# Top-32 attention and a quick-GELU MLP on one core: the end rows of a batch move in the work list, and MLP units are queued differently

## The chip, the core and the metric

The kernel runs on one core of a Trainium2 chip. The time is the device time of one execution in microseconds (us); the figure compared is the median of several runs. Every time below comes from the kernel before the change: its three timed runs, and one profiled execution.

The engines are named as in the profile: PE multiplies matrices (PEld is its weight load), DVE and POOL work elementwise on vectors, ACT applies functions and copies, SP issues nearly all DMA transfers from one queue, in program order.

## What is computed

Attention over 8 batches, 8 heads, 576 rows and 64 columns, in which only the 32 largest scores of a row count; then an MLP from 512 to 2048 to 512 columns over all 4608 rows.

```python
scores = scale * np.matmul(q, k.transpose(0, 1, 3, 2))
kth = np.partition(scores, -32, axis=-1)[..., -32:-31]
scores = np.where(scores >= kth, scores, -1e9)
attn = softmax(scores)
x = np.matmul(attn, v)          # then (B,H,S,D) -> (B*S, H*D)
h = x @ w_in
g = h * (1.0 / (1.0 + np.exp(-1.702 * h)))
out = g @ w_out
```

## The kernel before

**Slots.** The attention is a list of 144 slots (line 293), 18 for each of the 8 batches. A slot is 128 query rows of two heads (a head pair `hp`, of four). 576 rows are four full tiles of 128 and an end of 64, so a batch has 16 full slots, (tile, head pair), and two end slots; an end slot holds the last 64 rows of two head pairs at once. Before, every batch has its first three tiles (12 slots), then its two end slots, then its last tile (4 slots).

A slot passes these steps: `scores` on PE (line 303); `copy_scores` on ACT (319); `pair_up` and `topk` on DVE, called by `find` (328, 336, 956), which is most of DVE's time; `bounds` on POOL (361); `mask` and `exps` on ACT (375, 381); `normalize` on POOL (406); `split` (442), which ACT starts and SP ends by writing `rows` to DRAM; `turn_by_dma` (450), an SP transfer that brings the rows back transposed as `pt`; `values_at` on PE (504); `x_of` on ACT (522), which writes a part of the MLP's input `xT`. `pt` has two buffers, the scores `sc` four.

**Blocks and units.** When the last head pair of a tile is through, a block of 128 MLP rows is ready (`finish_x`, 534). The ends of two batches make one block, ready in the odd batch. There are 36 blocks of four units. A unit passes `hidden` on PE (562, called H below), `tanh` on ACT (581), `gate` (593), `combine` (610) and `project` on PE (657, called P below). `combine` makes four sums, `s1` to `s4`; `project` multiplies 28 small products, of which the first four read only the gated values and the fifth reads `s2`. Each of these steps has a queue, and a call takes the oldest unit that waits there, or does nothing. While slots run, `gate` and `combine` are POOL's; after the last slot they are DVE's.

**The order by hand.** Nothing is scheduled for the program: each engine runs its instructions in the order in which the code emits them. From slot 13 on, one call of `two_slots(n)` (1018) emits two slots' worth of work; n is odd, and "pair n" below is that call. On PE a full pair is H, H, scores(n+2), P, P, the values of slots n-3 and n-2, scores(n+3). After the last pair, `last_units` (1091) emits H, tanh, gate, combine and P of what is left.

**Due times.** `later` (733) holds work for a slot: loads of q, k and v, and the preparation of the next batch's q and k. `begin(0)` and `begin(1)` emit what is due at slots n and n+1; `prepare_some` emits preparations. From batch 2 on a preparation, `prepare_by_dma` (259), is a copy on ACT, four SP transfers to DRAM and, at `turns` (1044), one SP transposing transfer into `qk_t` (277). Batch 1 is prepared on PE (`prepare_by_pe`, 285). `READY`, `FETCH` and `VALUES` (741 to 745) say by head pair how many slots from the start of a batch this is due. One `load_v` (208) is three SP transfers.

Of the kernel before, what the change touches and what calls it, by code (L numbers as in the profile page):

```python
# [30 lines left out]
def kernel(  # L31
# [32 lines left out]
    NP = H // 2  # L64
# [24 lines left out]
    STEADY = PAIRED + 2  # L89
# [23 lines left out]
    ps_t = pool("ps_t", 2, space=PSUM)  # L113
# [118 lines left out]
    def turn_qk_ends(b, hp, ends):  # L232
        nc.tensor.transpose(ends, loaded.pop((b, hp))[1][:, 0, :, :], ident[:])
# [16 lines left out]
    def new_pair(b, hp):  # L250
        both = qkt.tile([P, 2 * S + TAIL], F32, name="qk_t")
        qT[b, hp], kT[b, hp] = both[:, 0:S], both[:, S : 2 * S + TAIL]
        return both
# [5 lines left out]
    def prepare_by_dma(b, hp):  # L259

        t = loaded.pop((b, hp))[2]
        halves = prp.tile([P, 2 * NF + 1, 2, P], U16, name="halves", tag="pr")
        words = t[:].rearrange("p c j d -> p c (j d)").bitcast(U16)
        nc.scalar.copy(out=halves[:], in_=words.rearrange("p c (e h) -> p c h e", h=2))
        rows = apart_qk.tile([2 * (S + TAIL), 2, P], U16, name="qk_rows")
        main = rows[:].rearrange("(g r) h e -> g r h e", g=2)[:, 0:FULL, :, :]
        for g in range(2):
            nc.sync.dma_start(
                main[g].rearrange("(t p) h e -> p t (h e)", p=P),
                halves[:, g * NF : (g + 1) * NF, :, :].rearrange("p t h e -> p t (h e)"),  # L270
            )
        nc.sync.dma_start(rows[FULL : FULL + P, :, :], halves[:, 2 * NF, :, :])
        nc.sync.dma_start(rows[2 * S : 2 * S + TAIL, :, :], halves[TAIL:P, 2 * NF, :, :])

        def turn():
            both = new_pair(b, hp)
            nc.sync.dma_start_transpose(
                out=both[:].bitcast(U16), in_=rows[0 : 2 * S + TAIL, :, :].rearrange("c h e -> (c h) e")
            )

        turns.append(turn)

    turns = []

# [8 lines left out]
    slots = []  # L293
    for b in range(B):

        full = [(b, t, (hp, hp)) for t in range(NF) for hp in range(NP)]
        ends = [(b, NF, (hp, hp + 1)) for hp in range(0, NP, 2)]
        slots += full[: -NP] + ends + full[-NP:]
    N = len(slots)
    PER = N // B  # L300
    st = [{} for _ in slots]
# [67 lines left out]
    def exponentials(n, between=lambda: None):  # L369

        mask(n)
        between()
        exps(n)
# [188 lines left out]
    def hidden(into=None):  # L562
        if not ready:
            return
        x = ready[0]
        fs, x.left = x.left[:G], x.left[G:]
        ph = ps_t.tile([P, G * P], F32, name="ph", tag="tp")[:] if into else both_banks[:, 0, :]
        for i, f in enumerate(fs):
            for c in range(CC):
                nc.tensor.matmul(  # L570
                    ph[:, i * P : (i + 1) * P],
                    lhsT=win[:, c, f * P : (f + 1) * P],
                    rhs=xs[:, x.place, c, :],
                    start=(c == 0),
                    stop=(c == CC - 1),
                )
        to_gate.append((ph, fs, x))
        if not x.left:
            free.append(ready.pop(0).place)

    def tanh(aside):

        if to_gate:
            ph, fs, x = to_gate.pop(0)
            th = thp.tile([P, G * P], F32, name="th")
            nc.scalar.activation(th[:], ph, AF.Tanh, scale=0.851 / RAISE)
            if aside:
                h = thp.tile([P, G * P], F32, name="h", tag="th")
                nc.scalar.copy(out=h[:], in_=ph)
                ph = h[:]  # L590
            gated.append((th, ph, fs, x, aside))
# [18 lines left out]
    def combine():  # L610

        if not to_combine:
            return
        th, h, fs, x, aside = to_combine.pop(0)
        if x.whole:
            return to_project.append((th, None, fs, x))
        sums = h if aside else thp.tile([P, G * P], F32, name="sums", tag="th")[:]
        engine = nc.gpsimd if aside else nc.vector
        g = th[:].rearrange("p (h c i r) -> p h c i r", h=2, c=2, i=2)
        s = sums.rearrange("p (s c r) -> p s c r", s=4, c=2)  # L620
        a11, a12, a21, a22 = g[:, 0, :, 0, :], g[:, 1, :, 0, :], g[:, 0, :, 1, :], g[:, 1, :, 1, :]
        s1, s2, s3, s4 = [s[:, i, :, :] for i in range(4)]
        engine.tensor_tensor(out=s1, in0=a21, in1=a22, op=ALU.add)
        engine.tensor_tensor(out=s2, in0=s1, in1=a11, op=ALU.subtract)
        engine.tensor_tensor(out=s4, in0=a12, in1=s2, op=ALU.subtract)
        engine.tensor_tensor(out=s3, in0=a11, in1=a21, op=ALU.subtract)
        to_project.append((th, (a11, a12, a22, s1, s2, s3, s4), fs, x))
# [25 lines left out]
    def sum_weights(count):  # L653
        for _ in range(min(count, len(summing))):
            summing.pop(0)()
# [66 lines left out]
    def merge_all(engine=nc.gpsimd):  # L722
        while merging:
            merging.pop(0)(engine)
# [10 lines left out]
    def at(n, fn, *args):  # L735
        later.setdefault(n, []).append((fn, args))
# [1 line left out]

    READY = (-13, -9, -5, -1)
    READY_1 = (-5, -5, -3, -1)
    FETCH = (-17, -13, -9, -5)
    FETCH_1 = (-11, -6, -4, -3)
    VALUES = (0, 1, 2, 3)
    by_slot = dict(enumerate([2, 2, 3, 3, 3, 3, 3, 3, 3, 3, 3, 1]))
    for n in by_slot:
        first = sum(map(len, list(by_slot.values())[:n]))
# [10 lines left out]
    for b in range(1, B):  # L759
        for hp in range(NP):  # L760
            if b > 1:
                for i, name in enumerate("qk"):
                    at(b * PER + FETCH[hp] + i, load, name, b, hp)
                at(b * PER + READY[hp], prepare_by_dma, b, hp)
            else:
                at(b * PER + FETCH_1[hp], load_both, b, hp)
                at(b * PER + READY_1[hp], prepare_by_pe, b, hp)
            at(b * PER + VALUES[hp], load_v, b, hp)
    unfinished = []
    early = []  # L770
    finished = []
# [4 lines left out]
    def may_project(waiting):  # L776

        return len(to_project) > waiting and len(finished) >= NG * CC + to_project[0][2][-1] + 1
# [188 lines left out]
    def project_one():  # L967
        if may_project(0):
            project(True)
# [48 lines left out]
    def two_slots(n):  # L1018

        begin, prepare_some = dues(n)  # L1020
        aside = n < N
        filling = n < STEADY + 8
        if live(n - 1):
            exponentials(n - 1)
        if n == STEADY or n > STEADY + 4:
            prepare_some()
        hidden(ps_t)
        hidden(ps_t)
        tanh(aside)
        if live(n + 2):  # L1030
            scores(n + 2)
        project_one()
        merge_all()
        combine()
        project_one()
        find(n, 8)
        if live(n - 1):
            normalize(n - 1)
            split(n - 1)
        gate()  # L1040
        begin(0)
        if live(n - 1):
            turn_by_dma(n - 1)
        while turns:
            turns.pop(0)()
        if live(n + 2):
            copy_scores(n + 2)
        if live(n):
            bounds(n)
            mask(n)  # L1050
        combine()
        sum_weights(4)
        if live(n):
            exps(n)
        tanh(aside)
        prepare_some()
        held = [m for m in (n - 3, n - 2) if live(m)]
        o = ps_t.tile([P, 4, P], F32, name="o", tag="tp") if held else None
        ends = [(b, hp, o[:, 2 + i, :]) for i, (b, hp) in enumerate(second_part)]
        second_part.clear()  # L1060
        for what in ends:
            turn_qk_ends(*what)
        for i, m in enumerate(held):
            values_at(m, o[:, i, :])
        if filling and held:
            x_of(held, o)
        for what in ends:
            copy_qk_ends(*what)
        if filling:
            begin(1)  # L1070
        if live(n + 3):
            scores(n + 3)
        leave_all()
        find(n + 1, 8)
        if live(n):
            normalize(n)
            split(n)
        if held and not filling:
            x_of(held, o)
        if not filling:  # L1080
            begin(1)
        if live(n):
            turn_by_dma(n)
        gate()
        if live(n + 3):
            copy_scores(n + 3)
        if live(n + 1):
            bounds(n + 1)
        sum_weights(4)
# [51 lines left out]
```

## Time and profile before

| What | us |
|---|---|
| Median of three runs (1436.27 to 1443.41) | 1436.47 |
| The profiled execution: its time | 1434.99 |
| The profiled execution: its span, first to last instruction | 1433.1 |
| PE busy in the span (96%) | 1374.1 |
| DVE busy (94%) | 1345.1 |
| ACT busy (81%) | 1165.1 |
| POOL busy (67%) | 959.3 |
| One top-8 search on DVE (`topk`, line 348), mean of 1080 | 0.596 |
| One transposing transfer into `pt`, median from issue to landing | 5.0 |
| One transposing transfer into `qk_t`, median from issue to landing | 5.3 |
| One write of `rows`, median from issue to landing | 3.5 |

The span is what the instructions fill; some 1.9 us lie around it in that execution. PE's ends are modelled, so a busy PE is one to which work was issued without a gap, not one at its peak; starts are what can be compared. The table of DMA issues counts SP's transfers, and the time that an issue holds the SP queue stands in the timeline of that queue.

### The profile page before, as it was taken

To read this page: it belongs to the slowest core of one execution; us is meant where nothing else is said; L and a number is where in the kernel's file an instruction comes from. 1 tells how busy PE (TensorE), PEld (TensorE's weight loads), DVE (VectorE), ACT (ScalarE), POOL (GpSimd) and SP (SyncE) were. 2 spreads that over 40 slices of the span, in tenths; PEclk is the share of its full clock that TensorE was granted. 3 is DMA by queue.
4 is the path that set the end of the run, shared out by engine and by line. 5 is a ranking of instruction groups with operands and counts; after the bars stand their busy time and mean duration, and the time that the engine had idled before them with its cause. 6 is when DMAs were issued, how large, how long until landed. Compare 5 with 4: busy or idle time off the path is not lost.

```text
span 1433.1 us, 45827 instructions
## 1 busy us (share of the span) xinstructions
PE 1374.1 (96%) x18164; PEld 1233.0 (86%) x18164; DVE 1345.1 (94%) x3526; ACT 1165.1 (81%) x1895; POOL 959.3 (67%) x1602
## 2 busy tenths in 40 slices
PE   6779797899999999999999999999999999999997
PEld 5667476799999999999999999999899999999997
DVE  7999998999999999999999999999999999999712
ACT  6998777888888888888888888888888888888811
POOL 4787694677766777777777777777666677777710
PEclk8899899999999999999999999999999999999999
DMA  7452465878687788778787887887887786655520
GB/s 223 141 152 72 126 155 151 195 189 195 169 203 184 192 192 201 202 182 187 190 208 180 187 196 182 198 190 189 185 208 189 182 205 175 175 141 141 141 58 16
DMA packets 535991, 245.47 MB, mean 171 GB/s; under 512 B 458976, under 2 KB 514273, under 8 KB 535777
## 3 DMA queue, kind: packets, MB, share of 16 engines
q1 hardware_dynamic: 535344, 242.25, 68.0%
q8 instruction: 142, 2.33, 0.7%
q14 instruction: 73, 0.59, 0.1%
q10 hardware_dynamic: 432, 0.30, 0.1%
HBM read 45.09 MB, written 103.42 MB: 104 GB/s over the span
## 4 chain that ended last, share of the span: by engine, by line
PE 81%; DVE 9%; ACT 4%; POOL 2%; DMA 2%; issue 1%; SPq 0%; POOLq 0%; ACTq 0%; DVEq 0%
PE ph L570 32%; PE po L677 28%; PE o L513 10%; PE s_ps L312 9%; DVE top L348 4%; DVE ranked L352 2%; DVE left L352 1%; DVE ranked L334 1%; DMA pt<-rows 1%; ACT pr L387 1%; DMA qk_t<-qk_rows 1%; PE tp L424 1%; POOL pr L410 1%; ACT sc L379 0%; PE po L570 0%
## 5 line engine op out<-in xcount | busy, mean ns | idle before, releaser
L348 DVE MAX8 top<-ranked 128x8 f32<-128x288 f32 (+1 forms) x1080 | 598.8, 596 | 0.0
L570 PEld LDWEIGHTS ph<-xT,win 128*128 128x128 f32 x4384 | 495.2, 192 | 32.1 <-ACT sc L446 14.9
L570 PE MATMUL ph<-xT,win 128*128 128x128 f32 x4384 | 509.2, 277 | 2.5 <-ACT xT L527 2.5
L352 DVE MATCH_REPLACE8 ranked<-top,ranked 128x288 f32<-128x288 f32 (+1 forms) x810 | 433.5, 543 | 0.0
L410 POOL TENSOR_SCALAR pr<-pr,rden 128x576 f32<-128x576 f32 x268 | 197.7, 749 | 319.2 <-DVE rden L397 196.1
L446 ACT COPY sc<-pr 128x2304 uint16<-128x2304 uint16 x134 | 283.5, 2116 | 130.9 <-POOL pr L410 130.5
L334 DVE TENSOR_TENSOR ranked<-sc 128x576 f32<-128x576 f32 x270 | 218.9, 852 | 3.2 <-ACT sc L324 3.2
L387 ACT ACTIVATE pr<-sc,low 128x576 f32<-128x576 f32 x288 | 220.3, 773 | 0.0
L379 ACT ACTIVATE sc<-sc,cut 128x576 f32<-128x576 f32 x288 | 207.8, 778 | 4.6 <-POOL cut L366 4.6
L677 PE MATMUL po<-raws,h 128*64 128x128 f32 x2048 | 198.8, 273 | 0.0
L677 PE MATMUL po<-wout,h 128*64 128x128 f32 x2048 | 198.8, 273 | 0.0
L324 ACT ACTIVATE sc<-s_ps 128x576 f32<-128x576 f32 x288 | 171.7, 650 | 21.7 <-PE s_ps L312 10.8
L312 PE MATMUL s_ps<-qk_t 64*64 64x288 f32 x2304 | 177.1, 420 | 3.8 <-ACT sc L324 2.2
L599 POOL TENSOR_TENSOR th<-th,h 128x512 f32<-128x512 f32 x130 | 166.5, 1281 | 10.8
L677 PE MATMUL po<-wout,th 128*64 128x128 f32 x2176 | 168.6, 276 | 0.0
L513 PE MATMUL o<-pt,v_l 128*64 128x128 f32 (+1 forms) x2400 | 146.8, 267 | 8.1 <-DMA pt<-rows 6.7
L677 PEld LDWEIGHTS po<-wout,th 128*64 128x64 f32 x2176 | 124.3, 137 | 28.2 <-issue 20.6
L513 PEld LDWEIGHTS o<-pt,v_l 128*64 128x64 f32 x2400 | 128.5, 140 | 9.9 <-DMA pt<-rows 7.3
L677 PEld LDWEIGHTS po<-raws,h 128*64 128x64 f32 x2048 | 129.5, 137 | 0.0
L677 PEld LDWEIGHTS po<-wout,h 128*64 128x64 f32 x2048 | 129.4, 137 | 0.0
L702 POOL TENSOR_TENSOR raws<-raws 128x128 f32<-128x128 f32 (+1 forms) x165 | 93.5, 575 | 47.3 <-ACT raws L695 39.5
L312 PEld LDWEIGHTS s_ps<-qk_t 64*64 64x64 f32 x2304 | 76.1, 134 | 52.9 <-issue 14.6
(106 smaller groups left out, 1725.0 us busy)
## 6 DMA issues: line engine op xcount, KB each, us to landing
rows<-sc SPq DMA_DIRECT2D x134, 576.0 KB, 3.5
qk_rows<-halves SPq DMA_DIRECT2D x48, 256.0 KB, 3.0
out_dram<-raws SPq DMA_DIRECT2D x136, 64.0 KB, 2.3
raws<-in_moe_w_in_dram SPq DMA_DIRECT2D x16, 512.0 KB, 4.4
v_l<-in_v_dram SPq DMA_DIRECT2D x32, 256.0 KB, 3.9
raws<-in_moe_w_out_dram SPq DMA_DIRECT2D x16, 512.0 KB, 3.5
qk_l<-in_q_dram SPq DMA_DIRECT2D x60, 128.0 KB, 3.4
qk_l<-in_k_dram SPq DMA_DIRECT2D x58, 128.0 KB, 3.5
```

The source lines that it names most:

```text
L312: nc.tensor.matmul(ps[i][rows, c, 0:HALF], lhsT=qT[b, hps[p]][on, cols], rhs=kT[b, hps[p]][on, FIRST[i] + c * HALF : FIRST[i] + (c + 1) * ...
L324: nc.scalar.mul(out=to, in_=ps[i][:, :, 0:HALF], mul=SCALE)
L334: nc.vector.tensor_tensor(out=ranked[n][:, :, c, :], in0=a, in1=b, op=op)
L348: nc.vector.max(top[:, i, 8 * r : 8 * r + 8], of(r, i))
L352: nc.vector.match_replace(to, top[:, i, 8 * r : 8 * r + 8], of(r, i), LOWEST)
L379: nc.scalar.activation(sc[:, i, :], sc[:, i, :], AF.Prelu, bias=cut[:, i : i + 1], alpha=HUGE)
L387: nc.scalar.activation(pr[:, i * S : (i + 1) * S], sc[:, i, :], AF.Exp, bias=low[:, i : i + 1], accum_out=den[:, i : i + 1],)
L410: nc.gpsimd.tensor_scalar(pr[:, i, :], pr[:, i, :], st[n]["rden"][:, i : i + 1], 1.0, op0=ALU.mult, op1=ALU.mult)
L446: nc.scalar.copy(out=halves, in_=pr[:].bitcast(U16).rearrange("p (k h) -> p h k", h=2))
L513: nc.tensor.matmul(o[j * D : (j + 1) * D, cols], lhsT=main[:, j, c, :] if c < NF else tail[:, j, :], rhs=pt[:, MAIN[j] + c if c < NF else ...
L570: nc.tensor.matmul(ph[:, i * P : (i + 1) * P], lhsT=win[:, c, f * P : (f + 1) * P], rhs=xs[:, x.place, c, :], start=(c == 0), stop=(c == C ...
L677: nc.tensor.matmul(both_banks[y * TAIL : (y + 1) * TAIL, bank, r * P : (r + 1) * P], lhsT=a[:, i, :], rhs=weight(w, fs[i])[:, y * P : (y + ...
```

## The change

- The two end slots come after the four tiles in an even batch and before them in an odd one, where before they came ahead of the last tile in both.
- For that, data of an odd batch are due at other times. The fourth head pair of q and k is prepared three slots ahead instead of one. The third is prepared when it was, but its transposing transfer is put off to three slots ahead (`at(..., turn)`). The four `load_v` of an odd batch, which were due at slots 0, 1, 2 and 3, are all due at slot 2. Batch 1 has its last preparation and load earlier too.
- In pairs 13 and 15 only one `hidden` is called instead of two.
- `prepare_some`, from pair 19 on, comes after `hidden` and `tanh`; two more calls stand at the later place.
- The two `project` calls of a pair stood together, the first ahead of `combine`. Now the first follows the pair's first `combine` and the second follows its second `combine`, which stands behind `bounds(n)`.

```diff
@@ prepare_by_dma
-        turns.append(turn)
+        if b % 2 and hp == 2:
+            at(b * PER + READY[1][3], turn)
+        else:
+            turns.append(turn)
@@ slots
-        slots += full[: -NP] + ends + full[-NP:]
+        slots += ends + full if b % 2 else full + ends
@@ due times
-    READY = (-13, -9, -5, -1)
-    READY_1 = (-5, -5, -3, -1)
+    READY = (-13, -9, -5, -1), (-13, -9, -5, -3)
+    READY_1 = (-5, -5, -3, -3)
     FETCH = (-17, -13, -9, -5)
-    FETCH_1 = (-11, -6, -4, -3)
-    VALUES = (0, 1, 2, 3)
+    FETCH_1 = (-11, -6, -4, -4)
+    VALUES = (0, 1, 2, 3), (2, 2, 2, 2)
...
-                at(b * PER + READY[hp], prepare_by_dma, b, hp)
+                at(b * PER + READY[b % 2][hp], prepare_by_dma, b, hp)
...
-            at(b * PER + VALUES[hp], load_v, b, hp)
+            at(b * PER + VALUES[b % 2][hp], load_v, b, hp)
@@ two_slots
-        if n == STEADY or n > STEADY + 4:
+        if n == STEADY:
             prepare_some()
         hidden(ps_t)
-        hidden(ps_t)
+        if n > STEADY + 2:
+            hidden(ps_t)
         tanh(aside)
+        if n > STEADY + 4:
+            prepare_some()
         if live(n + 2):
             scores(n + 2)
-        project_one()
         merge_all()
         combine()
         project_one()
...
         combine()
+        project_one()
         sum_weights(4)
         if live(n):
             exps(n)
         tanh(aside)
+        prepare_some()
         prepare_some()
```

## The prediction, made before the changed kernel was run

> **What bounds the kernel.** First the page: busy shares, slices, and the chain that ended last.
>
> ```profile
> PE 1374.1 (96%) x18164; PEld 1233.0 (86%) x18164; DVE 1345.1 (94%) x3526; ACT 1165.1 (81%) x1895; POOL 959.3 (67%) x1602
> ...
> PE   6779797899999999999999999999999999999997
> ...
> DVE  7999998999999999999999999999999999999712
> ...
> PE 81%; DVE 9%; ACT 4%; POOL 2%; DMA 2%; issue 1%; SPq 0%; POOLq 0%; ACTq 0%; DVEq 0%
> ```
>
> DVE is full until two slices before the end; PE has holes only in the first seven slices and works on alone at the end. So there are three stages: a filling one (to 295 us), a steady one, and a tail. The chain in order of time (start, us, what) shows the last two.
>
> ```profile
> 1292.88 7.34 PE ph L570 x64
> 1300.22 1.13 PE s_ps L312 x16
> 1301.36 6.26 PE po L677 x112
> 1307.62 2.18 PE o L513 x40
> 1309.80 1.13 PE s_ps L312 x16
> 1310.93 7.34 PE ph L570 x64
> ...
> 1377.63 3.77 PE ph L570 x32
> 1381.40 3.21 PE po L677 x56
> 1384.61 3.77 PE ph L570 x32
> ...
> 1416.28 9.35 PE po L677 x168
> ```
>
> A steady pair is H H 7.34, scores 1.13, P P 6.26, values 2.18, scores 1.13: 18.05 us with no gap. DVE's reciprocals come 8.84 us apart and every fourth time 9.56: (3 x 8.84 + 9.56)/2 = 18.04 a pair. PE has no slack, and what it waits for comes off nowhere else. In 295 to 1345 us PE has five such waits, 1.04 + 0.1 + 1.85 + 0.3 + 0.75 = 4.0 us, all for transposes (`pt`, `qk_t`).
>
> **Units.** I counted H and P in the order in which both programs issue them. Before, pair 19 has no H and pair 21 no P (the next block's last slots come late); after the last scores, 10 H and 14 P are left. After the change every pair from 17 on is full, and 9 H and 12 P are left. So one H and two P leave the tail for pairs 19 and 21. Total PE work is the same.
>
> *Tail.* After 1377.63 us it was five times 3.77 + 3.21, then 3.77 + 9.35: 48.0 us. One H and two P fewer are 3.77 + 2 x 3.12 = 10.0 less. But `last_units` emits H(u), gate(u), combine(u-1), P(u-1). Before, P took the unit combined a turn earlier; now it takes the one that this turn combines, on DVE behind gate(u), which follows H(u):
>
> ```profile
> 1382.07 0.69 DVE L601 SCALAR_TENSOR_TENSOR th<-th,ph 128x512 f32<-128x512 f32 x1 [11.47 <-ACT th L586]
> 1382.67 0.28 DVE L623 TENSOR_TENSOR sums<-th 128x128 f32<-128x128 f32 x1
> 1382.99 0.29 DVE L624 TENSOR_TENSOR sums<-sums,th 128x128 f32<-128x128 f32 x1
> ```
>
> H ended at 1381.40, `s2` at 1383.28. P's first four products (8 records of 0.056 = 0.45 us) need no sum; the fifth then waits 1.88 - 0.45 + about 0.15 to load its weights = 1.6 us. Behind it stands all of PE; nothing covers it. Five turns: 8.0 us; the last P is covered by the one before it. Tail: -10.0 + 8.0 = **-2.0** (bounds -10 if the sums come first, -0.5 at 1.9 a turn).
>
> *Second projection in steady pairs.* It now waits for the pair's second combine on POOL, which stands behind `bounds(n)`, so behind DVE's search; behind it on PE stand the values and scores(n+3), and for these ACT's copies and then DVE.
>
> ```profile
> 1283.29 0.21 POOL L366 TENSOR_SCALAR cut<-top 128x2 f32<-128x2 f32 x1
> ...
> 1284.14 0.46 POOL L624 TENSOR_TENSOR h<-h,th 128x128 f32<-128x128 f32 x1
> ```
>
> In that pair (H at 1274.76) P P begins at 1283.23, so the second half at 1286.40 and its `s2` product at 1286.85; the sum is ready at 1284.60: 2.2 us to spare. Over the steady pairs I find 1.2 to 2.6 us, once 0.3. Price 0; if the cover goes, some tenths each time. The first P moves behind the first combine, which ends 5.6 to 6.8 us before the second P would start where POOL merges a block first, and earlier elsewhere. POOL's order stays, since the same calls stand at the same places.
>
> **Filling stage.** From H of pair 17 (198.3) to H of pair 27 (295.04) before: 96.7 us. Five full pairs, with 0.15 more for each of two with end slots, are 90.5: -6.2. Pair 15 has one H less (-3.7), but 16 transposes at one place that wait for ACT; pair 17's P waits anyway for the weight sums (POOL L647 until 206.5). I take 0 there (+-2).
>
> **Moved loads.** In an odd batch, twelve transfers now stand together on SP ahead of pt(n), n = 18b+1. The same place before, b = 3:
>
> ```profile
> 570.42 0.57 SPq L448 DMA_DIRECT2D rows<-sc  x1
> 571.04 0.43 SPq L210 DMA_DIRECT2D v_l<-in_v_dram  x1
> 571.53 1.75 SPq L218 DMA_DIRECT2D v_e<-in_v_dram  x2
> 573.32 1.27 SPq L196 DMA_DIRECT2D qk_l<-in_k_dram  x2
> 574.63 1.55 SPq L199 DMA_DIRECT2D qk_l<-in_k_dram  x1
> 576.29 2.37 SPq L454 DMA_TRANSPOSE pt<-rows  x1
> ```
>
> SP is busy without a hole here. After 250 us a `v_l` holds SP for 0.51 on the mean (0.42 to 1.70), a `v_e` 0.80 (0.53 to 1.11): one `load_v` 2.25 with gaps (1.6 to 4.0), four 9.0 (6.3 to 16). The k load is 2.5. Counted from the end of the pair's values (566.0), when pt(54) may go: 0.1 + 2.6 (pt) + 0.6 (rows) + 9.0 + 2.5 + 2.4 (pt(55)) + 2.1 (landing) = 19.3. PE needs pt(55) after scores 1.13, H H 7.34, scores 1.13, P P 6.26 and one slot's values 1.09: 17.0. Late by **2.3 us** (-1 to +9), in batches 3 and 5: 4.6. Batch 7 has no k load: 0. In batch 1 (pair 19) loads stand even before `rows` (filling): 2.6 + 9.0 + 2.5 + 0.6 + 3.1 (landing) + 2.5 + 2.1 = 22.4, late by **5.4**. Behind the wait stand scores(n+3) and with them ACT and DVE. Before, PE waited 4.67 us for the same `pt`, and the granted clock of 236 to 274 us was 0.91; 20 value matmuls took 2.6 instead of 1.4. I add 1.4 for that. Filling: -6.2 + 5.4 + 1.4 = **+0.6**.
>
> The Trainium skill ("DMA: Bandwidth & Descriptors", Rules for kernel authors) advises to issue a transfer early and wait late, so that its fixed cost overlaps; by that v, needed a pair later, is free, and the sum would be some 10 us lower. The trace speaks against it: what costs is SP's time to issue. The skill ("TensorE: Matmul & The Clock Gate", Part 1) says that an idle window of about 3.4 us halves PE's clock; by it batch 1's wait costs more than itself and the waits of 2.3 do not, and at the upper bound those would, by about 2 us each.
>
> **The rest.** `prepare_some` behind `tanh`: ACT's 2.11 us copy starts 1.2 later; SP gets its four transfers 1.2 later, but waited anyway from 379.6 to 384.5 (pair 35) for PE's values: 0; without that gap, 1.2 each. The third head pair's transposing transfer (3 us on SP) falls into the same gap of 4.9 in pairs 51, 87, 123: 0; the fourth's `qk_t` arrived 0.1 to 1.9 us before its use, so without the gap 1 to 3 each. That POOL's merges and SP's stores leave the even batches' preparation pairs for the odd ones' moves waits, and I let the 4.0 stand (0 to 8).
>
> **Sum.** -2.0 + 0.6 + 4.6 = +3.2, on the profiled execution 1434.99 (span 1433.1 and 1.9 around): 1438.2; on the median, 1.5 higher: **1439.7 us**. I call 0.5% (7.2 us) what can be told from no change: same is 1429.3 to 1443.7.
>
> **Rivals.** *Loads hidden (faster).* SP issues at its minima (6.3 + 1.9 for loads and k): 16.0 after the values, pt(55) in time; pair 21 then waits 2.1 and no clock is lost; and the even batches' waits go (-4.0). 1439.7 - 4.6 - 4.7 - 4.0 = 1426. For it: 25 `v_l` with a median of 0.43. Against: SP runs into back-pressure where loads cluster. *SP overrun (slower).* Four loads take 15 us instead of 9: pt is late by 8.3, the next `rows` too, so that ACT's copy_scores waits for its `sc` buffer (it waited 1.07 us at 395) and DVE with it. Decisive from about 10 us, 1 us more in each of four batches; at 15 us it is 6 x 3 + 5.8 in batch 7 = +24: 1464; half of it, 1452. For it: issues at 1.7. Against: these are rare. *Double transpose (slower).* The third head pair's transfer does not fit in the gap and the fourth's comes 3 us late, with pt(n) behind: 3 batches x 3 = +9: 1449. Against: the gap. *Not what it says:* excluded for order, since PE's order shows the full pairs; that P waits in the tail does not depend on this.
>
> **Numbers.** The forecast's case (within 0.5%) 0.43; hidden loads 0.20; SP overrun 0.22; double transpose 0.15. So faster 0.20, same 0.43, slower 0.37. Range 1426 to 1453 (the overrun's worst and the best of the hidden loads lie outside); the forecast's own is 1430 to 1444.
>
> **What would show it.** Full pairs 19 and 21, H of pair 27 near 295.6; PE waits for `pt` in pairs 21, 57, 93 of 5.4, 2.3, 2.3 us and none at 129; five waits of 1.6 for DVE L624's counterpart in the tail. Wrong if steady pairs differ from 18.05, or if P waits for POOL in many of them.

## The result, and the profile after

| | before | after |
|---|---|---|
| Median of 11 runs each (lowest to highest), us | 1435.11 (1433.16 to 1443.41) | 1446.42 (1442.45 to 1451.53) |
| Ratio, 95% interval | | 1.0073 [1.0054, 1.0092] |
| The profiled execution: time / span, us | 1434.99 / 1433.1 | 1444.36 / 1442.4 |

The changed kernel is 0.7% slower. Measured again later beside other kernels (e8), it was 1439.09 against 1432.03 us: 1.0048 [1.0035, 1.0060]. Both say slower; the second interval lies about the 0.5% that the prediction drew as its line. The two occasions differ by more than chance: the eleven executions of the first took 1442.45 us and more, the five of the second 1441.51 and less.

The page of the changed kernel, busy time and the 40 slices:

```profile
PE 1380.9 (96%) x18164; PEld 1234.5 (86%) x18164; DVE 1343.8 (93%) x3521; ACT 1163.7 (81%) x1896; POOL 959.3 (67%) x1608
...
PE   6889799999999999999999999999999999999996
...
DVE  7999998999999999999999999999999999999812
```

The picture is that of before: the same number of matmuls, PE full but for the start, DVE done two slices before the end. An average does not find 10 us in 1440, so the stages are taken from the starts of H on PE (the first of each pair) and the end of the last P. The columns are stretches of time in us; "again" is e8's profiled execution, and the last two rows are the best kernel's two, which come below.

| | to H of pair 17 | 17 to 27 (filling) | 27 to 143 (steady) | 143 to last P (tail) | rest | span |
|---|---|---|---|---|---|---|
| before | 198.3 | 96.7 | 1050.9 | 79.6 | 7.5 | 1433.1 |
| after | 199.1 | 97.7 | 1060.3 | 78.0 | 7.2 | 1442.4 |
| after, again | 200.5 | 97.5 | 1052.6 | 78.6 | 7.2 | 1436.3 |
| e7 | 199.7 | 93.2 | 1051.7 | 69.6 | 7.2 | 1421.5 |
| e12 | 198.1 | 93.5 | 1050.9 | 70.1 | 7.2 | 1419.8 |

In the first execution the loss sits in the steady stage (+9.4, in the second +1.6), while the filling stage (+0.9) and the tail (-1.6) gain next to nothing by the one H and two P taken forward. The only trace of the kernel before is of the first occasion; on the second it took 1432.03 us and left no trace, so the second row's +3.2 explains a part of the 7.1 us that the medians show there.

**Tail.** The chain of the changed kernel that ended last, in order of time (start, us, what):

```profile
1388.74 3.78 PE ph L573 x32
1392.54 0.61 ACT th L589
...
1394.10 0.30 DVE sums L627
...
1394.44 2.95 PE po L680 x48
1397.39 3.78 PE ph L573 x32
```

Before, H and P alternated on PE alone (3.77 + 3.21 = 6.98). Now the chain leaves PE between H and P, for ACT's tanh and DVE's gate and sums: a turn is 1397.39 - 1388.74 = 8.65. The DVE timeline of the same turn shows gate, s1, s2 in the order in which `last_units` calls them:

```profile
1393.17 0.69 DVE L604 SCALAR_TENSOR_TENSOR th<-th,ph 128x512 f32<-128x512 f32 x1 [11.46 <-ACT th L589]
1393.78 0.28 DVE L626 TENSOR_TENSOR sums<-th 128x128 f32<-128x128 f32 x1
1394.10 0.29 DVE L627 TENSOR_TENSOR sums<-sums,th 128x128 f32<-128x128 f32 x1
```

The sum that P waits for does not need this gate, yet stands behind it.

**Steady stage.** SP's queue in the changed kernel at the values loads of batch 3 (the place that the prediction showed of before):

```profile
566.57 2.76 SPq L457 DMA_TRANSPOSE pt<-rows  x1
569.37 0.58 SPq L451 DMA_DIRECT2D rows<-sc  x1
570.00 0.43 SPq L210 DMA_DIRECT2D v_l<-in_v_dram  x1
570.47 1.73 SPq L218 DMA_DIRECT2D v_e<-in_v_dram  x2
...
577.65 1.10 SPq L218 DMA_DIRECT2D v_e<-in_v_dram  x2
578.81 1.26 SPq L196 DMA_DIRECT2D qk_l<-in_k_dram  x2
580.11 0.63 SPq L199 DMA_DIRECT2D qk_l<-in_k_dram  x1
580.79 4.16 SPq L457 DMA_TRANSPOSE pt<-rows  x1
585.04 2.69 SPq L714 DMA_DIRECT2D out_dram<-raws  x4
587.83 0.54 SPq L451 DMA_DIRECT2D rows<-sc  x1
```

Twelve values transfers hold SP from 570.00 to 578.75, then the next batch's k load, and only then pt(55) is issued. PE's timeline and, below it, the row of the view by windows for 588 to 592 us (the number after the five busy columns is the granted clock; it is 1.00 in the windows around) show what follows:

```profile
584.43 0.29 PE L516 MATMUL o<-pt,v_e 128*64 128x64 f32 x4
587.17 0.69 PE L516 MATMUL o<-pt,v_l 128*64 128x64 f32 x16 [2.45 <-DMA pt<-rows]
```

```profile
588.00:592.00 4.00, 4.00 (x42) 2.65 (x39) 2.11 (x9) 1.46 (x4) 1.29 (x3) 0.58 0.48 174
```

PE waits 2.45 us, and then its clock is half for 3.4 us: pair 57 takes 21.75 instead of 18.05. What else waits, in the view of waits (us in total, times, longest), first of the changed kernel, then three lines of before:

```profile
ACT sc L327 <- DMA rows<-sc: 19.1, 13, 5.1
...
PE o L516 <- DMA pt<-rows: 12.2, 7, 4.2
DVE ranked L337 <- ACT sc L327: 11.4, 6, 3.6
...
PE po L680 <- DVE sums L627: 6.8, 5, 1.4
...
ACT halves L264 <- DMA qk_l<-in_k_dram: 5.8, 3, 3.6
```

```profile
ACT sc L324 <- DMA rows<-sc: 8.7, 9, 1.8
...
PE o L513 <- DMA pt<-rows: 6.7, 3, 4.7
...
DVE ranked L334 <- ACT sc L324: 3.2, 3, 2.8
```

Three of these stand in no term of the prediction's sum. `copy_scores` on ACT waits for the writing of old `rows`, which stands in the same SP queue (8.7 us before, 19.1 after). DVE waits for that copy (3.2 and 11.4). These sums are of the whole run: of the 19.1 us 7.4 lie in pairs 21 and 23, and of DVE's 11.4 us 5.9 lie in the steady stage, in pairs 59, 95 and 123. And in odd batches ACT's preparing copy waits for a k load: the fourth head pair is now prepared two slots earlier, but its load is due when it was. That wait has DVE behind it, here in batch 7 (ACT's and DVE's timeline):

```profile
1183.21 2.11 ACT L264 COPY halves<-qk_l 128x2304 uint16<-128x2304 uint16 x1 [3.64 <-DMA qk_l<-in_k_dram]
```

```profile
1188.46 1.43 DVE L337 TENSOR_TENSOR ranked<-sc 128x576 f32<-128x576 f32 x2 [2.67 <-ACT sc L327]
```

By pairs, what goes beyond 18.05 us in the steady stage: 57, 59, 93 and 129 (behind the values loads) 6.95 us; 47, 69 and 97 (each a wait for `pt` in the pair after a preparation) 4.76; 125, behind the late k load of pair 123 and a `qk_t` that came 0.79 us late, 2.22; all of after 14.6, against 5.0 before. The POOL sums of steady pairs came in time, as predicted: P waited for them 0.2 us once.

### The profile page after: what moved, and what is told of

It is laid out like the page before. It is cut to its first block, busy times and chain, and to the rows that moved or that the text cites. A ratio compares the mean times of both kernels' runs of the same rounds, so it can differ in the third digit from the quotient of the medians.

```text
span 1442.4 us, 45910 instructions
## 1 busy us (share of the span) xinstructions
PE 1380.9 (96%) x18164; PEld 1234.5 (86%) x18164; DVE 1343.8 (93%) x3521; ACT 1163.7 (81%) x1896; POOL 959.3 (67%) x1608
## 3 DMA queue, kind: packets, MB, share of 16 engines
q8 instruction: 142, 2.33, 0.7%
## 5 line engine op out<-in xcount | busy, mean ns | idle before, releaser
L337 DVE TENSOR_TENSOR ranked<-sc 128x576 f32<-128x576 f32 x270 | 219.6, 854 | 11.4 <-ACT sc L327 11.4
L327 ACT ACTIVATE sc<-s_ps 128x576 f32<-128x576 f32 x288 | 171.5, 650 | 26.2 <-DMA rows<-sc 19.1
L315 PE MATMUL s_ps<-qk_t 64*64 64x288 f32 x2304 | 181.3, 429 | 1.1 <-DMA qk_t<-qk_rows 0.8
L516 PEld LDWEIGHTS o<-pt,v_l 128*64 128x64 f32 x2400 | 127.8, 140 | 14.2 <-issue 8.6
```

The source lines that it names most:

```text
L315: nc.tensor.matmul(ps[i][rows, c, 0:HALF], lhsT=qT[b, hps[p]][on, cols], rhs=kT[b, hps[p]][on, FIRST[i] + c * HALF : FIRST[i] + (c + 1) * ...
L327: nc.scalar.mul(out=to, in_=ps[i][:, :, 0:HALF], mul=SCALE)
L337: nc.vector.tensor_tensor(out=ranked[n][:, :, c, :], in0=a, in1=b, op=op)
L516: nc.tensor.matmul(o[j * D : (j + 1) * D, cols], lhsT=main[:, j, c, :] if c < NF else tail[:, j, :], rhs=pt[:, MAIN[j] + c if c < NF else ...
```

## The experiments

Each edit is made to the changed kernel, except where the text says otherwise. Ratios are to the kernel before on the same chip. e1 to e4 ran on one chip, e5 to e8 together, e9 and e10 together, e11 and e12 together.

**e1: the sums ahead of the gate in the tail**

```diff
@@ last_units
-        gate()
         combine()
+        gate()
         project_one()
```

> Only the tail differs from the changed kernel: a turn after the last slot runs combine ahead of gate, so that a P's sums no longer stand behind the gate of the unit just computed. Theory (the five turns of 8.65 us instead of 6.98 are waits for these sums): the turns go back to 6.98, 5 x 1.67 = 8.3 us less than the changed kernel, about 1438 where it has 1446 and the kernel before 1435 (ratio to before about 1.002). Rival (something else paces the tail, such as ACT or the single MLP buffers): turns stay above 8 us and the ratio stays at 1.006 to 1.009.

1431.62 us, 0.9996 [0.9985, 1.0007]. The chain of its tail:

```profile
1386.61 3.77 PE ph L573 x32
1390.37 3.21 PE po L680 x56
1393.58 3.77 PE ph L573 x32
```

PE is alone on the chain again, at 6.98 a turn. The stretch from H of pair 143 to the last P is 70.1 us instead of 78.0. Two calls in the wrong order cost five times 1.67 = 8.3 us, as the term of the prediction had it (8.0). The ratio fell by 0.0077 (11 us) against the first measurement of the changed kernel and by 0.0052 (7.4 us) against the second.

**e2: the odd batches' values loads behind pt(n)**

```diff
@@ dues
-                if fn not in preparing:
+                if fn not in preparing and not (fn is load_v and args[0] % 2):
...
+        def begin_late():
+            for fn, args in todo[1]:
+                if fn is load_v and args[0] % 2:
+                    fn(*args)
@@ two_slots, behind turn_by_dma(n)
+        begin_late()
```

> The four v loads of an odd batch are issued behind the pair's second pt transfer instead of ahead of it, in the same pair. Theory (the loads hold the SP queue and so make pt late): PE's waits in pairs 21, 57, 93 and 129 (4.16, 2.45, 1.02, 0.76 us, and the half clock after the first two, 2 to 3 us) go, and the time falls by 6 to 11 us, ratio to before 1.000 to 1.004. The next rows stay as late as they are, so the 2 us that ACT waits there for its score buffer stay. Rival (the queue's total load counts, not its order): the wait moves to the next pt or to the scores copy, and the ratio stays within 0.002 of the changed kernel's 1.0073.

1440.79 us, 1.0051 [1.0036, 1.0065]: between the two expectations, and no gain against the second measurement of the changed kernel. Pair 21 falls from 24.6 to 19.8 us, but the steady stage stays at 1061.5. Its waits:

```profile
ACT sc L327 <- DMA rows<-sc: 15.0, 7, 4.3
...
DVE ranked L337 <- ACT sc L327: 13.9, 8, 3.1
```

The waits for `pt` behind the values loads are gone, those for `rows` have grown longer each (15.0 us in 7 instead of 19.1 in 13), and DVE's behind them from 11.4 to 13.9. PE now waits 2.0 us for POOL in pair 59, and pair 59 takes 20.85 us. What is put behind one transfer of a full queue stands ahead of the next.

**e3: the fourth head pair's k load with its q load**

```diff
@@ due times, FETCH
-                    at(b * PER + FETCH[hp] + i, load, name, b, hp)
+                    at(b * PER + FETCH[hp] + (i if b % 2 == 0 or hp < 3 else 0), load, name, b, hp)
```

> In odd batches the k load of the fourth head pair is issued one slot earlier, with its q load. The changed kernel prepares this pair two slots earlier than before but loads it as before, and ACT's copy waited for the k load in batches 3, 5 and 7 (1.06, 1.06, 3.64 us), with DVE 0.7, 0.7 and 3.4 us late behind it. Theory (these waits cost PE up to 2.2 us in batch 7 and little in 3 and 5): the ACT waits go and the time falls by 1 to 4 us, ratio 1.005 to 1.007. Rival (DVE has room, or the moved load makes the pt behind it late instead): no change.

1439.21 us, 1.0047 [1.0029, 1.0066]. ACT's waits for a k load are gone (5.8 us to none). Against 1.0073 this is the gain expected, or a little more, against the 1.0048 of the second measurement none; alone it settles nothing. In pair 125 `qk_t` still came 1.77 us late, behind the third head pair's transposing transfer, and the clock halved: that pair took 22.1 us.

**e4: the unit order of before, with the changed slots and due times**

```diff
@@ two_slots
-        if n == STEADY:
+        if n == STEADY or n > STEADY + 4:
             prepare_some()
         hidden(ps_t)
-        if n > STEADY + 2:
-            hidden(ps_t)
+        hidden(ps_t)
...
-        if n > STEADY + 4:
-            prepare_some()
...
+        project_one()
         merge_all()
...
         combine()
-        project_one()
```

> The work list and due times of the changed kernel, with the pair of before: two H in pairs 13 and 15, both P ahead of the first and second combine, preparations at the head. Theory (the steady pairs are 18.05 us either way, and what the new unit order costs is in the tail): the tail has 8 H instead of 9 and no waits for sums, so 8.3 + 3.8 = 12 us less than the changed kernel, about 1434, ratio 0.998 to 1.001; PE's waits for pt in pairs 21, 57, 93 stay. Rival (the second P's wait for the pair's own combine paces steady pairs): more than 15 us less, with steady pairs below 18.05 us or the waits for pt gone.

1435.38 us, 1.0024 [1.0011, 1.0038]. The tail has 8 H and turns of 6.98; its stretch is 66.9 instead of 78.0 us. That is 11 us, and the time is only 3 to 7 us (0.0024 to 0.0049) below the changed kernel's. Against it stands a wait that only this kernel of the two has:

```profile
PE ph L573 <- ACT xT L530: 8.0, 7, 2.4
```

H waits for `x_of` 8.0 us in seven pairs. So the new order of units may have a use: with the slots moved, units taken as early as before run into the input that they read. What it takes is the tail's turn, which e1 gives back. This edit also puts the preparations back to the head of the pair, and the share of that is not separated. The reverse, the new unit order on the slots of before, was not tried.

**e5: the next batch's first k load a pair later**

```diff
@@ due times, FETCH
-                    at(b * PER + FETCH[hp] + i, load, name, b, hp)
+                    at(b * PER + FETCH[hp] + (2 * i if b % 2 == 0 and hp == 0 else i), load, name, b, hp)
```

> The changed kernel, but the k load of the next (even) batch's first head pair is due a pair later, so that in pairs 19, 55, 91 it no longer stands on SP between the four values loads and pt(n). Theory (what costs at this place is SP's time to issue): pt(n) comes 2.5 us sooner. The waits of PE for pt in pairs 57 and 93 (2.45 and 1.02 us) and the half clock at 588.7 go, pair 57 takes about 18.1 and not 21.75, pair 59 18.1 and not 18.8, pair 93 18.2 and not 19.4; the wait in pair 21 falls from 4.16 to about 1.7 and pair 21 from 24.6 to about 21 to 22. Sum -6 to -8 us, ratio to the kernel before 1.0073 - 0.005 = 1.002. Rival (the waits only move, as they did when the values loads were put behind pt): the k load now stands ahead of pt(n+1) and of a rows write, ACT's copy of the scores waits as long for its buffer, and pair 59 or the preparation behind it takes what pair 57 gave; ratio 1.005 to 1.007.

1432.52 us, 1.0004 [0.9993, 1.0016]; the changed kernel beside it 1439.09. That is 6.6 us for one load moved. SP's queue at the same place:

```profile
568.26 0.42 SPq L210 DMA_DIRECT2D v_l<-in_v_dram  x1
...
575.76 1.10 SPq L218 DMA_DIRECT2D v_e<-in_v_dram  x2
576.91 2.41 SPq L457 DMA_TRANSPOSE pt<-rows  x1
579.42 3.75 SPq L714 DMA_DIRECT2D out_dram<-raws  x4
583.26 0.55 SPq L451 DMA_DIRECT2D rows<-sc  x1
583.86 1.52 SPq L196 DMA_DIRECT2D qk_l<-in_k_dram  x2
```

pt(55) is issued 12.1 us after pt(54), not 14.2, and holds SP for 2.41 and not 4.16; the k load stands behind the `rows` write. Pairs 57, 59 and 93 have no wait left (18.2, 18.05, 18.2 us), pair 21 takes 18.96 and the 6.8 us of half clock after it are gone; ACT waits 5.6 us for `rows` instead of 19.1 (15.9 in e8). Theory held; the rival's moved wait did not come. What the traces show of the gain lies in the filling stage, where the same four loads stand in pair 19: 93.0 us against 97.5 in e8, with pair 21 at 18.96 instead of 24.42. The steady stage of this execution (1054.5) lies between the two of the changed kernel. The waits of ACT for the fourth k load stayed (8.0 us), with pairs 53 and 125 at 20.3 each.

**e6: e1 and e3 together** (both diffs as above)

> Both single edits that gained, together: in the tail the sums go ahead of the gate, and the k load of an odd batch's fourth head pair is due with its q load. Theory (one works in the tail, the other in the steady stage, and they share nothing): the gains add up, 0.9996 - 0.0026 = 0.997 of the kernel before; tail turns 6.98 us, and no wait of ACT for a k load. Rival (the gain of the early k load came from waits that happened to fall elsewhere in that execution): 0.9995, as with the tail alone.

1429.83 us, 0.9984 [0.9973, 0.9995], between the two. Beside the changed kernel (1.0048) this is 0.0064, of which the tail's 8.3 us are 0.0058. In this execution pairs 57 and 125 waited 2.66 and 2.33 us, each with a half clock of 3.4 us behind it. The early k load frees ACT; that with SP's queue still full the next wait takes its place fits this, but is not shown by one execution.

**e7: e1, e3 and e5 together**

```diff
@@ due times, FETCH
-                    at(b * PER + FETCH[hp] + i, load, name, b, hp)
+                    at(b * PER + FETCH[hp] + (0 if b % 2 and hp == 3 else 2 * i if b % 2 == 0 and hp == 0 else i), load, name, b, hp)
@@ last_units
-        gate()
         combine()
+        gate()
```

> The tail's sums ahead of the gate, the fourth head pair's k load early, and the next batch's first k load a pair later. Theory (all three add up): 0.997 - 0.005 = 0.992 of the kernel before, 10 to 12 us less than it; from the first full pair on at most 8 us beyond 18.05 a pair up to the last pair with scores. Rival (the relief at the values loads only moves waits): 0.996 to 0.997, as without the third edit.

1421.64 us, 0.9921 [0.9907, 0.9934]: the three add up, and this beats both kernels. Its waits:

```profile
ACT sc L327 <- DMA rows<-sc: 10.2, 9, 2.8
...
DVE ranked L337 <- ACT sc L327: 3.0, 4, 1.5
PE o L516 <- DMA pt<-rows: 2.9, 4, 1.1
```

By the table of stages it is 11.6 us below before: tail 10.0, filling 3.5, steady -0.8, the start -1.4, the rest 0.3. Here the moved H and two P bring the full 10.0 us that the prediction counted for them.

**e8: the changed kernel again**

> The changed kernel once more, on the chip of the other runs of this call. Theory: ratio 1.0073 as before, with tail turns of 8.65 us; of the steady stage's waits those for pt in pairs 57 and 93, for the k load in pairs 53, 89 and 125 and the late qk_t in pair 125 come again, each within 1 to 2 us of its size. Rival (they are chance, and the difference is the tail's alone, which is 8.3 us against 10.0 us of work less): the steady stage comes out as in the kernel before, within 2 us, and the ratio below 1.003.

1439.09 us, 1.0048 [1.0035, 1.0060]. Neither expectation fits whole. Turns of 8.65, the waits for `pt` in pairs 57 (1.97 us) and 93 (0.42), and the k load's (1.80 and 1.10 us, in batches 3 and 7) came again; pair 125 took 18.75 instead of 20.27, pair 97 18.39 instead of 20.72. The steady stage is 1.6 us above the trace of before, not 9.4. Without the half clock after a wait, and with most waits shorter, most of the steady loss goes: its size changes between executions.

**e9: the edit of e5, made to the kernel before**

> The kernel before, with the one edit that gave the changed kernel back 6 us: the k load of the next (even) batch's first head pair a pair later. Theory (the edit pays by what the change put on SP at that place; before, SP had room there, and PE's waits for pt were 4.0 us in the whole steady stage, none over 0.75 us in the pairs that follow 19, 55 and 91 but for 1.85 in pair 103): ratio 0.998 to 1.001; what it gives lies before the first full pair, where PE waited 4.67 us for a pt. Rival (the load was badly placed in both kernels, and the gain has nothing to do with the change): 0.994 to 0.996.

1432.54 us, 1.0007 [0.9998, 1.0016]: no gain. (The pair that the expectation calls 103 is 105, since pair 19 has no H in this kernel.) The k load's place was no fault of the kernel before; it became one when all four values loads were put in front of it, where one had stood.

**e10: e7 and e2 together**

> The three edits that added up (sums ahead of the gate, fourth k load early, next k load a pair later: 0.9921), and the values loads of odd batches behind pt(n) besides. Theory (SP's queue is full at this place, so that only what leaves it helps, and what is merely put behind moves its wait to the next pair's rows and pt): no gain, 0.992 to 0.995, with waits of ACT for rows writes and of P for POOL in pairs 59 and 131 where e7 has waits for pt in pair 57. Rival (each wait for pt that is taken away counts): 0.990, as the waits for pt in pairs 25, 39 to 57 and 93 (2.9 us) go.

1429.07 us, 0.9982 [0.9973, 0.9991], worse than both expectations and 0.006 of the time behind e7 (0.9921):

```profile
ACT sc L327 <- DMA rows<-sc: 16.1, 8, 4.6
...
DVE ranked L337 <- ACT sc L327: 10.2, 6, 3.5
```

DVE's idle time behind the late copies is 10.2 us, where e7 has 3.0. PE waits for POOL in pairs 23, 95 and 131 (1.56, 0.52 and 0.93 us). Keeping PE from waiting for `pt` by making `rows` late is a bad bargain, as DVE is as full as PE.

**e11: e1 and e5 together, without the early k load**

> The sums ahead of the gate and the next batch's first k load a pair later, without the early k load of the fourth head pair. Theory (ACT's wait for the late fourth k load, 1.1 to 4.0 us in each of batches 3, 5 and 7 with DVE behind it, costs 3 to 4 us): 0.9945 to 0.9955 of the kernel before, as 1.0004 of the single edit less 0.0058 for the tail's 8.3 us says too, and 3 to 5 us above the kernel with all three edits on the same chip. Rival (that wait is one of those that fall elsewhere when it is taken away; the tail with the early k load was only 0.0006 below the sum of the changed kernel's 1.0048 and the tail's 0.0058): 0.992 to 0.993, within 1.5 us of the kernel with all three.

1425.90 us, 0.9950 [0.9933, 0.9967]. The wait that e12 has not:

```profile
ACT halves L264 <- DMA qk_l<-in_k_dram: 8.3, 3, 3.8
```

**e12: e7 again, beside e11**

> The three edits once more, beside the same kernel without the early k load. Theory: 0.992 of the kernel before, as in the first measurement [0.9907, 0.9934]. Rival (that measurement of five executions was a lucky one): 0.995 or more, near the 0.9945 of the sum of the single edits.

1421.63 us, 0.9932 [0.9920, 0.9943], so e7's gain came again. The early k load is thus worth 4.3 us at the median once SP's queue is relieved, as the theory of e11 says (the intervals of e11 and e12 overlap by 0.001); in e11 ACT waits for it 3.53, 0.98 and 3.80 us, and pairs 53 and 125 take 20.3 each, in e12 18.4 and 19.0.

## Why the prediction came out as it did

The median of 1446.42 us lies 6.7 us above the predicted 1439.7 and inside the range of 1426 to 1453, which the rivals had made wide; the forecast's own 1430 to 1444 it misses. The likeliest case was "within 0.5%", and what came was slower: 0.73% and, again, 0.48%. Against the first profiled execution's +9.4 the sum said +3.2. Step by step:

- **Tail, -2.0.** Measured from the first H of `last_units` to the last P: 48.0 before, 1435.1 - 1388.7 = 46.4 after, so -1.6. Right, and so were its parts: 10.0 of work less, and five turns longer by 1.67 (1.6 predicted), which e1 takes away.
- **Second projection in steady pairs, 0.** Right: undisturbed pairs still take 18.05.
- **Filling, +0.6.** Measured +0.9, and +0.8 to +2.2 ahead of pair 17, which had been taken as 0 (+-2). PE waited 4.16 us for pt(19), not 5.4, with the half clock that was added: pair 21 took some 2.2 us beyond that wait, where the prediction allowed 1.4, so that two errors offset each other in part. e5, e7 and e12 show what the full pairs alone would bring: the stretch falls to 93.0 to 93.5.
- **Values loads, +4.6.** Their time on SP was right: 9.0 us predicted, 8.2 to 8.8 measured. The waits were 2.45, 1.02 and 0.76 us for 2.3, 2.3 and 0, so 4.2 in all; but the first brought a half clock with it, which the prediction had excluded at 2.3 us, and a late `rows` behind it (pair 59). By pairs the term measured 6.95, in the second execution 3.3.
- **"I let the 4.0 stand."** In the first execution this is the step that failed. The waits outside the values loads were carried over from before, with a bound of 0 to 8 and no cause. There was one to be seen in the diff: `READY` moved the fourth head pair from -1 to -3, and `FETCH` did not move with it, so that the copy came right behind its load. ACT waited 5.8 us for it, DVE behind ACT. Outside the values loads the steady pairs lost 7.6 us (14.6 - 6.95) for 5.0 before; 2.2 of the 2.6 more are pair 125, behind the longest of these waits. That the wait is the cause there is not shown: in e3, without it, pair 125 took 22.1. In the second execution, with 2.9 us of such waits, the same pairs lost 3.5, less than before, and the term held. e11 and e12 put the price of the late load at 4.3 in the kernel whose queue is relieved.
- **Third head pair's transposing transfer, 0.** In pair 123 it went ahead of pt, and the fourth's `qk_t` came 0.79 us late in pair 125; in e3 1.77, with a half clock. Small, not nothing.
- **Behind the late pt.** The prediction named what stands behind a wait for `pt` on PE, but let only PE's wait into the sum. The same queue carries `rows`, and their lateness reaches ACT and DVE without PE (ACT's waits went from 8.7 to 19.1 us, DVE's behind them from 3.2 to 11.4). The overrun rival had that mechanism, with a threshold of 10 us of loads; it set in below it, at 8.2 to 8.8.

On the page's advice quoted in the prediction ("DMA: Bandwidth & Descriptors", Rules for kernel authors: issue early, wait late, and the fixed cost overlaps), the runs are plain: the values arrived in time in both traced executions of the changed kernel, and it was SP's time to issue them that cost. e5 moves one load out of a full place and gains 6.6 us; e2 issues values later and is no faster than e8 (1.0051 and 1.0048).

What stays open: why the steady stage of one kernel differs by 8 us between two occasions, whose times do not overlap. The waits there are of the size of SP's own variation (at the same place one transposing transfer held it for 4.16 us in the first and for 3.31 in the second), and a half clock comes or doesn't, by where a wait falls (below); what made the transfers slower on the first occasion is not known.

## What to carry to other kernels

Where one queue issues everything, cost a moved transfer by what then stands behind it in that queue, and follow each of those to its waiter, on every engine, not only to the one that is fullest: the same k load was free before and cost over 6 us once twelve transfers stood ahead of it. When the due time of a step moves, look for the due time of what feeds it, and move that too. A unit delayed on purpose in a loop takes the cover with it in the loop's tail: look there for the one call whose order must change.

## What the runs showed of the hardware

- **The half clock goes by how much of a wait falls into one step of a grid.** Single waits of PE of 2.45 (after), 3.03 (e1), 2.66 and 2.33 (e6), 2.39 (e4) and 1.77 us (e3) were followed by a granted clock of half for 3.4 us; waits of 2.24 (e1), 2.20 (after), 2.09 (e9), 1.97 (e8) and 1.95 us (e5) were not. Within a run, the half clock begins on one grid of 3.413 us: in the changed kernel at 254.15 and 588.66 us, 98 steps apart. Counted by these steps from 295 to 1380 us in all fourteen traces, PE was idle for 1.77 to 2.33 us in the six steps that a half clock followed, and for at most 1.78 us in every other. PE's ends are modelled, so the two figures are as good as equal: the limit lies near half a step here. The wait of 2.45 us put 1.92 into one step, and the next one has half the clock (length, busy time of PE, PEld, DVE, ACT and POOL, granted clock):

```profile
585.25:588.66 3.41, 1.49 (x44) 1.46 (x48) 3.41 (x10) 2.15 (x2) 3.17 (x7) 1.00 0.79 181
588.66:592.08 3.42, 3.42 (x23) 2.14 (x20) 1.45 (x6) 1.48 (x4) 0.71 (x2) 0.50 0.48 184
```

  e1's wait of 2.24 us at the same place lay across a line of the grid, 0.98 and 1.25 us, and the clock stayed:

```profile
581.35:584.77 3.42, 2.43 (x64) 2.29 (x60) 3.39 (x9) 1.57 (x5) 1.79 (x3) 1.00 1.08 121
584.77:588.18 3.41, 2.16 (x56) 1.79 (x56) 3.41 (x11) 2.21 (x2) 3.17 (x7) 1.00 0.88 274
588.18:591.59 3.41, 3.41 (x36) 3.12 (x29) 2.50 (x7) 2.53 (x5) 0.47 (x2) 1.00 0.41 72
```

  The Trainium skill ("TensorE: Matmul & The Clock Gate", Part 1) gives an idle window of about 3.4 us that runs freely. The grid and the length of each dip agree; but about half a window without work set it off here. The prediction's reading of that page, that 2.3 us is safe, was wrong.
- **A transposing transfer's hold on SP varies.** Over a whole run it is 2.5 to 2.6 us at the median for `pt`. In batch 3, behind the twelve loads and a k load, it was 4.16 (after), 3.32 (e4), 3.31 (e8), 3.15 (e3), 2.99 (e6) and 2.75 us (e1), and 2.29 to 2.42 where the k load was away (e5, e7, e11, e12). In batches 1 and 5 the same runs have 2.30 to 2.83 with the k load and 2.17 to 3.16 without, so that the k load is not shown to lengthen it.
